# A fused state-space and MLP block on one core: first weights in four pieces, one broadcast held back, the opening of the matmul engine rearranged, and a new hand-written order of all steps

## The chip, the core and the metric

The kernel runs on one core of one Trainium2 chip. The metric is the device time of one execution in microseconds (us), as the median of several runs. One further execution was recorded by the hardware profiler; all durations below come from it.

## What is computed

The input x is one sequence of 2048 rows of 448 numbers in bfloat16. It is normalized once, and the normalized rows go two ways: through a diagonal complex state-space recurrence (a scan over the 2048 rows), and through a second normalization and a two-layer MLP of width 1792. The two are multiplied and added to x.

```python
xn = _layernorm(x, axis=-1)
s = _A_ref(xn, ...)        # Bu = xn @ B_bar.T ; h = Lam_bar*h + Bu ; y = 2*Re(h @ C.T) + xn*Dskip
g = _silu(_B_ref(xn, ...)) # _layernorm(xn), gelu(y @ w1 + b1) @ w2 + b2
return x + s * g
```

## The kernel before, in words

The 2048 rows are cut into eight blocks (x0 to x7) of 256 rows, and a pair of blocks makes a group g = 0 to 3. A partition holds two neighbouring rows of a block (par 0 and 1), so one block is two tiles of 128 rows. The recurrence is run over pairs of rows: 256 steps per group, each step advancing two rows.

Per group the work is this. The statistics of the four tiles are taken on VectorE (lines 357 and 361), turned into two scales and two offsets (`ln_scale`, lines 388 to 412; on GpSimd for groups 1 to 3, as five instructions with a power function, or on VectorE as eleven small ones), and applied (line 421 on VectorE or 422 on ScalarE) to give xn (for the recurrence) and xm (for the MLP). Both are turned by transposing DMAs on SyncE's queue (`xt`, line 435, shown at line 83) into xnT and xn2T. Only block 0 and the MLP side of block 1 are transposed on TensorE instead (lines 379 and 437). Then TensorE makes: `bu` (line 613), the input of the recurrence, in four parts i = 0 to 3; `mm1` (line 683), the first MLP layer, in seven parts j = 0 to 6 of two times 128 hidden units, each followed by a gelu on ScalarE (690); `mm2` (line 714), the second layer, in four tiles, each followed on VectorE and ScalarE by lines 717, 718 and 719; and `ym` (lines 746, 749 and 752), the output of the recurrence, in four tiles, each followed on VectorE by lines 755 and 758 and by the output DMA. The recurrence (`ssm`, lines 627 to 672) is a long VectorE chain between `bu` and `ym`: three wide products and sums, seven scans (638), three wide ones again; the last results h and hh are what `ym` reads. For group 0 `mm1` is done in halves, one block at a time (`mm1_half`, line 699), so that it can begin as soon as block 0 is there.

Before the loops, small parameters are made (`parameters`, mostly on GpSimd), B is scaled and transposed (`lb` line 564/566 and `bt` line 582, giving the tiles BT0 to BT6), C is loaded and transposed (`ldc`, `ct_dma`, giving Cr) and combined into CQ and CZ (`cq`, again lines 564/566), and M0 is made from CQ (`m0`, line 602). The vector b2 and the skip vector (dbc) are broadcast to all partitions by two DMAs that GpSimd issues (lines 336 and 337); dbc is then halved (338).

w1 (448 x 1792) is loaded in two halves of columns, each as a piece of 384 rows and one of 64 rows (`ldw1`); `fcol` picks the 128 columns of one part with a stride of 7, which fits how w2 is loaded, seven rows to a partition and half. Row 64 of the last quarter of w1_sb holds b1.

Nothing is scheduled while the kernel runs. Every step is a `Task` with the names that it reads and writes. `link` derives what must come before what; `emit` writes the steps to the engines' queues in the order of the list `ORDER`, so an engine does its steps strictly in the order of that list, and waits at a step until what it needs is done. `SECOND` lists the steps that may run on either of two engines and take the second one. The numbers `dur` and `prio` in the code are not used by `emit`; they belong to the program that searched the order. The steps are numbered as the code adds them, so a change that adds steps renumbers all later ones.

In the opening, TensorE does 28 dummy products of the identity (line 777), nine tiny ones for the parameters (453 to 457), eight more dummies, the eight transposes of block 0, and then `mm1_half`. SyncE issues, in order: x0 in two pieces, w1 first half in two pieces, b1, x1, w1 second half in two pieces, B in four, w2 in two, x2 and x3 in one, C in three, and then the transposing DMAs.

The rule by which TensorE's steps in the opening are made:

```python
for n, each, rd, pri in ((28, 0.1, [], 2 * PINNED), (8, 0.06, ["ps7"], 2 * PINNED + 1)):
    pe([lambda e: e.matmul(psum[:, 3, 0:128], ident[:, :], ident[:, :], start=True, stop=True) for _ in range(n)],
       ["ident"] + rd, ["ps3"], n * each, pri)
```

Of the kernel before, what the change touches and what calls it, by code (L numbers as in the profile page):

```python
# [8 lines left out]
ALU = mybir.AluOpType  # L9
# [130 lines left out]
def dram_ap(t, offset, ap):  # L140
    return bass.AP(tensor=t.tensor, offset=offset, ap=ap)
# [5 lines left out]
0 11 18 22 12 1 9 10 19 23 14 83 16 20 24 17 2 15 5 21 25 13 27 3 26 7 8 85 6 28 4 86 29 91 40 87 30 92 84 88 93 31 89 41 94 32 43 42 44 90 48 97 95  # L147
45 33 49 47 96 50 34 59 99 108 46 51 100 110 57 109 101 102 98 35 103 52 112 58 111 53 114 113 39 137 104 116 115 105 176 140 136 106 60 117 138 55 61
118 56 139 107 177 54 141 62 120 175 146 63 119 148 67 163 64 122 142 164 65 144 68 121 161 124 69 66 147 123 71 149 126 77 150 125 81 70 152 143 128
78 154 72 74 127 153 130 73 151 129 79 36 162 132 131 303 82 155 134 75 302 76 178 266 80 307 133 305 135 309 165 167 304 145 308 306 168 310 270 179  # L150
267 156 166 171 181 169 157 172 274 180 158 170 37 314 311 315 271 316 159 312 227 160 313 278 268 38 183 272 269 282 228 275 173 273 182 285 229 317
279 318 186 174 283 280 362 230 281 184 392 320 284 231 363 321 188 286 276 364 185 232 287 277 235 319 233 365 236 366 187 234 395 237 322 368 245
367 241 189 191 243 370 369 244 192 193 323 240 371 194 195 372 197 413 324 415 374 419 417 373 196 199 200 325 375 412 416 414 203 380 418 198 420
326 204 201 238 215 239 327 202 246 213 216 205 248 421 422 328 376 424 425 219 430 206 220 255 223 256 431 257 329 214 258 259 207 381 330 224 388
377 382 208 427 383 378 242 428 379 249 247 209 250 426 389 251 252 217 253 390 384 218 254 423 210 260 221 261 222 211 262 225 472 332 212 226 474
263 473 264 385 265 331 386 288 475 333 338 476 336 334 341 478 477 289 335 342 480 479 339 340 344 482 387 337 481 391 345 291 346 343 290 347 348
349 484 350 483 292 429 293 351 393 295 352 485 356 502 357 394 294 490 296 190 358 353 354 355 359 360 297 298 491 492 486 299 361 432 523 522 526
527 525 398 487 529 488 524 528 489 433 530 399 493 494 300 434 396 505 400 397 531 534 535 401 495 536 532 496 540 435 402 541 403 405 503 404 436
497 504 537 301 538 437 406 539 600 408 438 407 441 439 542 442 498 440 533 443 446 543 450 447 449 570 544 451 448 545 571 499 455 456 444 457 453
445 458 572 452 459 460 409 546 467 574 461 573 410 462 463 466 464 454 465 547 468 575 469 576 411 470 548 471 500 552 578 577 551 553 549 579 556  # L160
580 550 561 558 582 581 554 555 559 508 501 583 562 560 564 584 557 509 563 510 506 603 511 566 585 588 512 586 513 587 507 565 515 567 568 592 589
514 569 590 516 517 591 596 593 601 594 602 595 518 597 598 609 519 599 606 520 610 521 604 611 613 605 607 608 612 617 614 621 615 618 616 619 622
620 623 624
""".split()]
SECOND = [int(k) for k in """
138 141 142 143 167 171 173 197 199 217 223 284 311 318 320 393 395 396 421 422 424 425 428 503 505 506 507 532 534 535 538 541 603
# [12 lines left out]
def bass_recurrent_scan__ssm_conv_s5__mixer_channel_mlp__prompt_kernel(  # L179
# [18 lines left out]
    with ExitStack() as es:  # L198
# [63 lines left out]
        def pool(fn, reads=(), writes=(), dur=0.3, prio=0):  # L262
            kb.add("pool", fn, reads, writes, dur=dur, lat=0.15, prio=prio)
# [7 lines left out]
        def pe(fn, reads=(), writes=(), dur=0.2, prio=0):  # L271
            kb.add("pe", fn, reads, writes, dur=dur, lat=0.25, prio=prio)

        with nc.Block():
# [28 lines left out]
            def ld(eng, o, i, writes, nbytes, prio, reads=(), dur=0.45):  # L303
                kb.dma(eng, o, i, reads=reads, writes=writes, prio=prio, nbytes=nbytes, dur=dur)
# [8 lines left out]
            NW1 = 2  # L313

            def ldw1(c, prio):
                w = F // NW1
                ld("sp", w1_sb[:, 0:3, c * w:(c + 1) * w],
                   dram_ap(B_w1, c * w, [[F, 128], [128 * F, 3], [1, w]]), [f"w1_{c}"], 384 * w * 2, prio, dur=0.55)
                ld("sp", w1_sb[0:64, 3, c * w:(c + 1) * w], dram_ap(B_w1, 384 * F + c * w, [[F, 64], [1, w]]),
                   [f"w1r_{c}"], 64 * w * 2, prio)  # L320
# [7 lines left out]
            ldw1(1, S1 + 3)  # L328
# [4 lines left out]
            for q in range(2):  # L333
                ld("sp", w2_sb[:, q * 7:q * 7 + 7, :],
                   dram_ap(B_w2, q * 7 * 128 * D, [[7 * D, 128], [D, 7], [1, D]]), [f"w2_{q}"], 650000, S1 + 6, dur=1.7)
            ld("pool", b2bc[:], dram_ap(B_b2, 0, [[0, 128], [1, D]]), ["b2bc"], 114688, -50, reads=["sgn3"])
            ld("pool", dbc[:], dram_ap(A_Dskip, 0, [[0, 128], [1, D]]), ["dbc"], 114688, -20, reads=["b2bc"])
            pool(lambda e: e.tensor_scalar(dbc[:], dbc[:], 0.5, None, op0=ALU.mult), ["dbc"], ["dbc"], 0.8, -20)
# [10 lines left out]
            def xk(b):  # L349
                return [f"x{b}"] if b else ["x0p0", "x0p1"]  # L350
# [13 lines left out]
            def first_norm():  # L364

                for par in range(2):
# [13 lines left out]
                                                                       ident[:, :]) for d in range(4)], [f"xm0p{par}", "ident"], [f"ps{bank}"], 0.33, 2 * PINNED)  # L380
# [293 lines left out]
            def fcol(fi):  # L674

                q, t = divmod(fi, 7)
                return slice(q * 896 + t, q * 896 + 896, 7)

            def mm1(g, j, prio):
# [6 lines left out]
                w = F // NW1  # L686
                cs = sorted({(2 * j * 128) // w, ((2 * j + 2) * 128 - 1) // w})
# [5 lines left out]
            def mm1_half(j, b, k3, prio):  # L693
# [9 lines left out]
                w = F // NW1  # L703
                ws = sorted({(2 * j * 128) // w, ((2 * j + 2) * 128 - 1) // w})
# [5 lines left out]
            def mm2(g, b, par, prio):  # L710
# [5 lines left out]
                pe(fns, [f"gT{gb}_{fi}_{b}" for fi in range(NF)] + ["w2_0", "w2_1"], [f"ps{bk}"], 2.66, prio)  # L716
# [16 lines left out]
            def ym(g, b, par, prio):  # L733
# [9 lines left out]
                def part(c0, c1):  # L743
# [7 lines left out]
                    else:  # L751
# [6 lines left out]
                    dve(lambda e: e.tensor_tensor(o_sb[:, ob, par * D + c0:par * D + c1], t3[:, fb, c0:c1], res, ALU.add),  # L758
                        [f"t3{fb}_{c0}", f"t3{fb}_256"] + ([f"xr{b}"] if par else xk(2 * g + b)), [f"o{ob}_{par}_{c0}"], 0.1 + (0.28, 0.47)[par] * w / D, prio)
                    if last:  # L760
                        kb.dma("sp", dram_ap(out, off + par * D + c0, [[2 * D, 128], [1, w]]), o_sb[:, ob, par * D + c0:par * D + c1], reads=[f"o{ob}_{par}_{c0}"],
                               writes=[f"out{g}{b}{par}{c0}"], prio=prio, nbytes=256 * w)
# [13 lines left out]
            for n, each, rd, pri in ((28, 0.1, [], 2 * PINNED), (8, 0.06, ["ps7"], 2 * PINNED + 1)):  # L776
                pe([lambda e: e.matmul(psum[:, 3, 0:128], ident[:, :], ident[:, :], start=True, stop=True) for _ in range(n)],
                   ["ident"] + rd, ["ps3"], n * each, pri)
# [85 lines left out]
```

## Time and profile before

| what | value |
|---|---|
| median of 4 runs | 161.85 us (161.48 to 162.73) |
| the profiled execution's own time | 162.0 us |
| its span | 160.2 us |
| TensorE busy (line "PE") | 151.9 us, 95% |
| VectorE busy (DVE) | 132.9 us, 83% |
| ScalarE busy (ACT) | 92.7 us, 58% |
| GpSimd busy (POOL) | 56.6 us, 35% |
| TensorE clock granted | 0.999 |
| read from memory | 6.89 MB |

Times in the views are counted from the start of the span. In the views of an engine a row gives the start, the length, the engine and line, the operation, what it writes and reads, how many instructions were merged, and in brackets how long the engine stood idle just before and what ended that. "SPq" is SyncE issuing a DMA: the length of such a row is the issue, not the transfer. A view of one line or tile also gives the time from issue to landing. Rows overlap a little, because an instruction's start and the end of the one before are recorded in pipelined form. Line 83 and line 84 are the helper lines of all transposing and all other DMAs, so their rows are told apart by the tile. "xn_sb" in a row can be xn or xm, "w_sb" w1 or w2, "tmp" also the output tile.

### The profile page before, as it was taken

Reading aid. Unit: us, or ns where it says so; the run is one execution under the profiler, and the core shown is the slowest. Engines: PE = TensorE matmul, PEld = TensorE weight load, DVE = VectorE, ACT = ScalarE, POOL = GpSimd, SP = SyncE. Lnnn points to the kernel's source line nnn. Section 1 sums busy time; section 2 is a strip of 40 time slices with the busy share of each in tenths; the row PEclk is TensorE's granted clock in tenths of the full one; section 3 lists DMA queues with packets and bytes.
Section 4 is the critical chain, followed back from the end, with each engine's and each line's share of the span. In section 5 each row is a group of like instructions: output and inputs, shape, how many; then the busy total and the mean of one; then the engine's idle time right before and its main releaser. Section 6 shows DMA issues by size and latency. Waiting matters only on the chain.

```text
span 160.2 us, 2700 instructions
## 1 busy us (share of the span) xinstructions
PE 151.9 (95%) x944; PEld 97.8 (61%) x944; DVE 132.9 (83%) x254; ACT 92.7 (58%) x152; POOL 56.6 (35%) x132
## 2 busy tenths in 40 slices
PE   6899999959999999999999999999999999999990
PEld 6789955646666665555565556567677665555560
DVE  5588878469799899699993999997989899896763
ACT  3769897949887894956289211344279678111100
POOL 5568939098200433300012843632046000005230
PEclk9999999999999999999999999999999999999999
DMA  4999999999882006000000811062601000010021
GB/s 99 339 322 383 265 157 202 115 141 178 158 151 76 0 0 131 4 0 0 0 0 16 214 34 29 0 179 58 123 4 57 0 4 0 3 54 0 27 87 59
DMA packets 29926, 14.70 MB, mean 92 GB/s; under 512 B 24597, under 2 KB 29593, under 8 KB 29914
## 3 DMA queue, kind: packets, MB, share of 16 engines
q1 hardware_dynamic: 29810, 14.31, 39.9%
q0 software_dynamic: 96, 0.23, 1.1%
q8 instruction: 7, 0.11, 0.3%
q14 instruction: 5, 0.04, 0.1%
q10 hardware_dynamic: 8, 0.00, 0.0%
HBM read 6.89 MB, written 1.84 MB: 54 GB/s over the span
## 4 chain that ended last, share of the span: by engine, by line
PE 74%; DMA 12%; DVE 4%; SPq 4%; POOL 2%; issue 1%; ACT 0%; DVEq 0%
PE psum L683 23%; PE psum L714 20%; PE psum L613 12%; PE psum L746 12%; DMA x_all<-in_A_x_dram 8%; SPq L84 4%; DMA xn2T<-xn_sb 4%; PE psum L749 4%; PE psum L602 3%; DVE lnst L357 1%; POOL lnw L400 1%; DVE t L755 1%; PE psum L752 1%; DVE xn_sb L421 1%; DVE tmp L758 1%
## 5 line engine op out<-in xcount | busy, mean ns | idle before, releaser
L714 PE MATMUL psum<-w_sb,gT 128*128 128x448 bf16 x224 | 44.5, 352 | 0.0
L683 PE MATMUL psum<-xn2T,w_sb 128*128 128x512 bf16 x168 | 38.1, 380 | 1.8 <-DMA xn2T<-xn_sb 1.8
L714 PEld LDWEIGHTS psum<-w_sb,gT 128*128 128x128 bf16 x224 | 21.8, 98 | 19.4
L683 PEld LDWEIGHTS psum<-xn2T,w_sb 128*128 128x128 bf16 x168 | 21.8, 132 | 15.0 <-DMA xn2T<-xn_sb 2.1
L690 ACT ACTIVATE gT<-psum 128x1024 bf16<-128x1024 f32 x21 | 21.5, 1022 | 11.5 <-PE psum L683 11.4
L613 PE MATMUL psum<-xnT,BT 128*128 128x256 bf16 x196 | 24.0, 273 | 0.0
L613 PEld LDWEIGHTS psum<-xnT,BT 128*128 128x128 bf16 x196 | 19.0, 98 | 5.4 <-ACT u_sb L617 0.5
L718 ACT ACTIVATE th<-o 128x448 f32<-128x448 f32 x16 | 9.1, 573 | 20.6 <-DVE o L717 20.5
L755 DVE TENSOR_TENSOR t<-psum,g_sb 128x448 bf16<-128x448 f32 (+2 forms) x17 | 10.1, 592 | 5.6 <-PE psum L752 3.9
L638 DVE TENSOR_TENSOR_SCAN s_f<-cw,cur,v_sb 128x256 f32<-128x256 f32 x21 | 14.4, 734 | 0.2
L719 DVE SCALAR_TENSOR_TENSOR g_sb<-th,o 128x448 bf16<-128x448 f32 x16 | 10.9, 683 | 4.3 <-ACT th L718 4.3
L699 PE MATMUL psum<-xn2T,w_sb 128*128 128x256 bf16 x112 | 12.8, 273 | 0.9 <-DVE xn2T L381 0.6
L730 POOL TENSOR_TENSOR xr<-xd,g_sb 128x448 f32<-128x448 bf16 x4 | 4.5, 1120 | 24.8 <-DVE g_sb L719 20.9
L699 PEld LDWEIGHTS psum<-xn2T,w_sb 128*128 128x128 bf16 x112 | 12.1, 132 | 1.3 <-DVE xn2T L381 0.8
L421 DVE TENSOR_SCALAR xn_sb<-x_all,lnw 128x448 bf16<-128x448 bf16 x20 | 10.3, 534 | 2.1 <-POOL xd L730 1.4
L746 PE MATMUL psum<-CZ,h_sb 128*128 128x448 bf16 x56 | 11.9, 352 | 0.0
L717 DVE TENSOR_TENSOR o<-psum,b2bc 128x448 f32<-128x448 f32 x16 | 9.9, 618 | 1.7 <-PE psum L714 1.6
L617 ACT ACTIVATE u_sb<-psum 128x512 bf16<-128x512 f32 x12 | 7.1, 592 | 6.8 <-PE psum L613 6.8
L746 PE MATMUL psum<-CQ,h_sb 128*128 128x448 bf16 (+2 forms) x54 | 10.5, 332 | 0.0
L422 ACT ACTIVATE xn_sb<-x_all,lnw 128x448 bf16<-128x448 bf16 x10 | 7.5, 755 | 5.1 <-DVE xn_sb L421 3.7
L357 DVE BATCH_NORM_STATS2 lnst<-x_all 128x6 f32<-128x448 bf16 x14 | 8.2, 611 | 1.9 <-DMA x_all<-in_A_x_dram 1.9
L706 ACT ACTIVATE gT<-psum 128x512 bf16<-128x512 f32 x14 | 8.1, 594 | 2.5 <-PE psum L699 2.4
(154 smaller groups left out, 222.6 us busy)
## 6 DMA issues: line engine op xcount, KB each, us to landing
w_sb<-in_B_w_dram SPq DMA_DIRECT2D x2, 784.0 KB, 9.3
out_dram<-tmp SPq DMA_DIRECT2D x7, 224.0 KB, 1.9
w_sb<-in_B_w_dram SPq DMA_DIRECT2D x2, 672.0 KB, 5.6
x_all<-in_A_x_dram SPq DMA_DIRECT2D x3, 448.0 KB, 3.8
gT<-in_A_C_re_dram SPq DMA_DIRECT2D x1, 392.0 KB, 13.0
Bn<-in_A_B_re_dram SPq DMA_DIRECT2D x1, 336.0 KB, 6.6
Bn<-in_A_B_im_dram SPq DMA_DIRECT2D x1, 336.0 KB, 6.7
gT<-in_A_C_im_dram SPq DMA_DIRECT2D x1, 336.0 KB, 12.9
```

The lines of the kernel that those rows point to most:

```text
L357: dve([lambda e, b=b, par=par, q=q: e.bn_stats(lnst[:, q, :], x_all[:, 2 * g + b, par, :])], [f"x{2 * g + b}"] + (["xmT0p1"] if (g, b) == ...
L421: on = [("dve", lambda e: e.tensor_scalar(dst, src, rs, nb, op0=ALU.mult, op1=ALU.add), 0.4, 0.12), ("act", lambda e: e.activation(dst, sr ...
L613: fns = [lambda e, r=r, m=m, d=d: e.matmul(psum[:, 4, r * NK:(r + 1) * NK], BT[:, m, d, :], xnT[:, gx, d, :], start=(d == 0), stop=(d == 6 ...
L638: dve(lambda e, i=i, ri=ri, init=init: e.tensor_tensor_scan(s_f[:, i, ri, :], col(R2, i).to_broadcast([128, NK]), v_sb[:, i, ri, :], init, ...
L683: fns = [lambda e, k=k, d=d: e.matmul(psum[:, b0 + k, :], w1_sb[:, d, fcol(2 * j + k)], rhs[:, d, :, :], start=(d == 0), stop=(d == 3)) fo ...
L690: act(lambda e: e.activation(gT[:, gb, 2 * j:2 * j + 2, :], psum[:, b0:b0 + 2, :], ACT.Gelu_apprx_tanh), [f"ps{b0}", f"ps{b0 + 1}"] + (WK ...
L699: fns = [lambda e, k=k, d=d: e.matmul(psum[:, banks[k], :].rearrange("p (r c) -> p r c", r=2)[:, :, cs], w1_sb[:, d, fcol(2 * j + k)], rhs ...
L714: fns = [lambda e, fi=fi: e.matmul(psum[:, bk, 0:D], gT[:, gb, fi, q * 128:(q + 1) * 128], w2_sb[:, fi, :], start=(fi == 0), stop=(fi == N ...
L717: dve(lambda e: e.tensor_tensor(o2[:, fb, :], psum[:, bk, 0:D], b2bc[:], ALU.add), [f"ps{bk}", "b2bc"], [f"oo{fb}"], 0.62, prio - 76)
L719: dve(lambda e: e.scalar_tensor_tensor(out=g_sb[:, gs, :], in0=th[:, fb, :], scalar=1.0, in1=o2[:, fb, :], op0=ALU.add, op1=ALU.mult), [f" ...
L746: fns = [lambda e, k=k: e.matmul(psum[:, bk, c0:c1], h_sb[:, hb, k, k0:k0 + 128], cm[:, k, c0:c1], start=(k == 0), stop=False) for k in ra ...
L755: dve(lambda e: e.tensor_tensor(t3[:, fb, c0:c1], psum[:, bk, c0:c1], g_sb[:, gs, c0:c1], ALU.mult), [f"ps{bk}", f"g{gs}"], [f"t3{fb}_{c0} ...
```

## The change

Six things are edited.

1. w1 is loaded in four pieces of 4, 4, 4 and 2 times 128 columns (`CH`), each again as 384 and 64 rows; w2 in four pieces to match. `fcol` takes a stride of 4 (2 in the last). A part of `mm1` now waits for its own piece alone; `mm2` waits for all four of w2.
2. The broadcast of b2 also waits for the last piece of w1 (`w1r_3`).
3. The first four transposes follow the parameter products at once, then come five dummies, the other four transposes, and five more dummies. The eight dummies are gone.
4. Halving dbc may run on ScalarE or VectorE instead of GpSimd (it takes VectorE).
5. At the end, the last tile's second addition may run on GpSimd, and its output DMA is issued by ScalarE; the additions of a tile wait for their own part only, where before the first also waited for the second's product.
6. `ORDER` and `SECOND` are new from end to end.

The code, without the two lists:

```diff
-            NW1 = 2
+            CH = ((0, 4), (4, 4), (8, 4), (12, 2))
+            chunk = [c for c, (_, n) in enumerate(CH) for _ in range(n)]
             def ldw1(c, prio):
-                w = F // NW1
-                ld("sp", w1_sb[:, 0:3, c * w:(c + 1) * w],
...
+                a, w = CH[c][0] * 128, CH[c][1] * 128
+                ld("sp", w1_sb[:, 0:3, a:a + w], dram_ap(B_w1, a, [[F, 128], [128 * F, 3], [1, w]]), [f"w1_{c}"], 384 * w * 2, prio, dur=0.55)
+                ld("sp", w1_sb[0:64, 3, a:a + w], dram_ap(B_w1, 384 * F + a, [[F, 64], [1, w]]), [f"w1r_{c}"], 64 * w * 2, prio)
...
-            ldw1(1, S1 + 3)
+            for c in (1, 2, 3):
+                ldw1(c, S1 + 3)
...
-            for q in range(2):
-                ld("sp", w2_sb[:, q * 7:q * 7 + 7, :],
-                   dram_ap(B_w2, q * 7 * 128 * D, [[7 * D, 128], [D, 7], [1, D]]), [f"w2_{q}"], 650000, S1 + 6, dur=1.7)
-            ld("pool", b2bc[:], dram_ap(B_b2, 0, [[0, 128], [1, D]]), ["b2bc"], 114688, -50, reads=["sgn3"])
+            for c, (a, n) in enumerate(CH):
+                ld("sp", w2_sb[:, a:a + n, :], dram_ap(B_w2, a * 128 * D, [[n * D, 128], [D, n], [1, D]]), [f"w2_{c}"], 98000 * n, S1 + 6, dur=0.5 + 0.1 * n)
+            ld("pool", b2bc[:], dram_ap(B_b2, 0, [[0, 128], [1, D]]), ["b2bc"], 114688, -50, reads=["sgn3", "w1r_3"])
...
-            pool(lambda e: e.tensor_scalar(dbc[:], dbc[:], 0.5, None, op0=ALU.mult), ["dbc"], ["dbc"], 0.8, -20)
+            kb.either(("act", lambda e: e.activation(dbc[:], dbc[:], ACT.Copy, scale=0.5), 0.6, 0.2),
+                      ("dve", lambda e: e.tensor_scalar(dbc[:], dbc[:], 0.5, None, op0=ALU.mult), 0.2, 0.12), ["dbc"], ["dbc"], -20)
...
+                    pe([lambda e: e.matmul(psum[:, 3, 0:128], ident[:, :], ident[:, :], start=True, stop=True) for _ in range(5)],
+                       [f"xm0p{par}", "ident"], ["ps3"], 0.3, 3 * PINNED + 1)
...
-                q, t = divmod(fi, 7)
-                return slice(q * 896 + t, q * 896 + 896, 7)
+                a, n = CH[chunk[fi]]
+                return slice(a * 128 + fi - a, (a + n) * 128, n)
...
-                    dve(lambda e: e.tensor_tensor(o_sb[:, ob, par * D + c0:par * D + c1], t3[:, fb, c0:c1], res, ALU.add),
-                        [f"t3{fb}_{c0}", f"t3{fb}_256"] + ([f"xr{b}"] if par else xk(2 * g + b)), [f"o{ob}_{par}_{c0}"], 0.1 + (0.28, 0.47)[par] * w / D, prio)
+                    add = lambda e: e.tensor_tensor(o_sb[:, ob, par * D + c0:par * D + c1], t3[:, fb, c0:c1], res, ALU.add)
+                    rd = [f"t3{fb}_{c0}", f"t3{fb}_256"] if c0 == 0 and not (last and par) else [f"t3{fb}_{c0}"]
...
+                    if last and par:
+                        kb.either(*on, rd, [f"o{ob}_{par}_{c0}"], prio)
...
-                        kb.dma("sp", dram_ap(out, off + par * D + c0, [[2 * D, 128], [1, w]]), o_sb[:, ob, par * D + c0:par * D + c1], reads=[f"o{ob}_{par}_{c0}"],
+                        kb.dma("act" if c0 else "sp", dram_ap(out, off + par * D + c0, [[2 * D, 128], [1, w]]), o_sb[:, ob, par * D + c0:par * D + c1], reads=[f"o{ob}_{par}_{c0}"],
...
-            for n, each, rd, pri in ((28, 0.1, [], 2 * PINNED), (8, 0.06, ["ps7"], 2 * PINNED + 1)):
+            pe([lambda e: e.matmul(psum[:, 3, 0:128], ident[:, :], ident[:, :], start=True, stop=True) for _ in range(28)],
+               ["ident"], ["ps3"], 2.8, 3 * PINNED)
```

Counted out step by step, the new lists give these queues, as far as the prediction speaks of them. SyncE: x0, w1 piece 0, b1, x1, w1 pieces 1 to 3, B in four, w2 in four, x2 and x3, two of the three pieces of C, then the transposes BT3, the last piece of C, xnT of block 1, BT0, xnT of block 0, xm of block 2, xm of block 3, the four of C, x4 and x5, BT4, BT1, x6 and x7, BT5 and so on. TensorE after the opening: `mm1_half` for block 0 (the transposes of block 1 behind part 5), for block 1, the four `mm2` of group 0, one `bu` of group 0, all seven `mm1` of group 1 in a row, the next `bu` of group 0, three `mm2` of group 1, and then `m0`, `bu`, `mm2` and `mm1` of group 2 by turns up to the first `ym`. GpSimd: the b2 broadcast now stands in front of 20 small parameter steps and the broadcast of dbc directly behind them, where before the scales of group 1 stood in front of it. VectorE: the scales of group 1 (moved from GpSimd), all four xm of group 1, the halving of dbc, and the recurrence of group 0, which now stands behind nearly all of CQ and CZ. At the end TensorE makes the smaller part (columns 256 to 447) of the last tile before the larger.

## Prediction

> **What bounds the kernel now.** I read the page first: the engines' shares, then the slices.
>
> ```profile
> PE 151.9 (95%) x944; PEld 97.8 (61%) x944; DVE 132.9 (83%) x254; ACT 92.7 (58%) x152; POOL 56.6 (35%) x132
> ...
> PE   6899999959999999999999999999999999999990
> ...
> DVE  5588878469799899699993999997989899896763
> ...
> PEclk9999999999999999999999999999999999999999
> DMA  4999999999882006000000811062601000010021
> ```
>
> TensorE is busy from start to end, at full clock, with a dip in the ninth slice; transfers fill the first twelve slices. So the time is TensorE's work plus the places where it does not run, plus what comes after it. TensorE's timeline names the places:
>
> ```profile
> 5.15 1.03 PE L777 MATMUL psum<-ident 128*128 128x128 bf16 x8
> 5.98 0.82 PE L379 MATMUL psum<-ident,xn_sb 128*128 128x128 bf16 x8
> 7.42 2.83 PE L699 MATMUL psum<-xn2T,w_sb 128*128 128x256 bf16 x24 [0.63 <-DVE xn2T L381]
> 10.55 1.93 PE L699 MATMUL psum<-xn2T,w_sb 128*128 128x256 bf16 x16 [0.30 <-DMA w_sb<-in_B_w_dram]
> ...
> 36.22 1.94 PE L683 MATMUL psum<-xn2T,w_sb 128*128 128x512 bf16 x8 [1.78 <-DMA xn2T<-xn_sb]
> ```
>
> Useful work starts at 7.42; then it stops 0.30 us for the second half of w1 and 1.78 us for the transposed xm of group 1; after 38 us the waits list no stop of TensorE over 0.2 us. How that transpose came late is in SyncE's and GpSimd's timelines:
>
> ```profile
> 14.07 7.00 SPq L83 DMA_TRANSPOSE xnT<-xn_sb  x1
> ...
> 28.60 3.40 SPq L83 DMA_TRANSPOSE xn2T<-xn_sb  x2
> 32.05 4.14 SPq L83 DMA_TRANSPOSE BT<-Bn  x2
> ```
> ```profile
> 27.69 0.64 POOL L84 DMA_DIRECT2D dbc<-in_A_Dskip_dram  x1
> ```
>
> The first transpose was stuck 7 us in its issue, until the loads had drained at 21. A transpose otherwise takes 1.3 us of issue and lands after 3.0 to 3.3; the two for xm of group 1, issued just after the dbc broadcast, landed after 6.0 and 6.3. The broadcast itself lands at 32.2.
>
> The end, in VectorE's timeline:
>
> ```profile
> 154.87 0.62 DVE L755 TENSOR_TENSOR t<-psum,g_sb 128x448 bf16<-128x448 f32 x1 [1.10 <-PE psum L749]
> 155.53 0.39 DVE L758 TENSOR_TENSOR tmp<-t,x_all 128x448 bf16<-128x448 bf16 x1
> 155.84 0.42 DVE L755 TENSOR_TENSOR t<-psum,g_sb 128x256 bf16<-128x256 f32 x1
> 156.29 0.42 DVE L758 TENSOR_TENSOR tmp<-t,xr 128x256 bf16<-128x256 bf16 x1
> 156.75 0.36 DVE L755 TENSOR_TENSOR t<-psum,g_sb 128x192 bf16<-128x192 f32 x1
> 157.14 0.36 DVE L758 TENSOR_TENSOR tmp<-t,xr 128x192 bf16<-128x192 bf16 x1
> ```
>
> Six VectorE steps without a pause, then an output DMA.
>
> **The opening.** The parameter products end at 5.15, and the first tile is normed at 4.75 (VectorE: 4.39 plus 0.36). So its transposes run 5.15 to 5.57 (eight took 0.82). Five dummies at 0.104 (eight filled 5.15 to 5.98) reach 6.09, the second four transposes 6.50. Before, transposes ended at 6.80 and the work began at 7.42, so 0.62 later; now 7.12 to 7.15. Gain **0.27**. Dummies behind the last transposes lie in the wait for the copy. Ends: 0 if weights or b1 are then late, 0.5 if the copy of the first tile, now off that path, shortens it more.
>
> **w1 in four pieces.** Six more issues on SyncE (four of w1, two of w2) at about 0.48 us: B moves 1.9 us back, x2 and x3 from 8.27 to about 11.1. Is that paid? Bytes in the order of issue: x0 0.23 MB, piece 0 0.46, x1 0.23, pieces 1 to 3 1.15, B 0.8, w2 1.6, x2 and x3 0.46. The stretches show 0.40 MB moved by 4 us, 1.75 by 8, 3.04 by 12, 4.2 by 15, 5.0 by 17. By 8.4 us 2.6 MB are issued and 1.9 moved; at 11 all 4.5 MB, against 2.7 moved. The queue does not run dry: cost 0. Pieces land 1.0 to 1.4 us behind their bytes (w1's second half: 2.06 MB pass at 8.9, landed 10.3). So piece 1 lands near 8.1 and is needed at 8.9 (two parts of 0.88), piece 2 near 9.7 against 10.7, piece 3 near 10.4 against 12.9. The 0.30 goes: gain **0.30**. Against this stands the Trainium skill, "DMA: Bandwidth & Descriptors", section "Rules for kernel authors": for bandwidth, at least 1 MiB per DMA, and its measured table gives 64 KB a third of the peak. If each of six more DMAs paid the 2.0 us which that page fits as fixed, one behind the other, x2 and x3 would land 12 us later. The rows say otherwise: the stretches of 1 us between 4 and 14 us move 237 to 401 GB/s with pieces of 56 to 784 KB in the queue, because several are in flight. I take 0; bounds -0.3 to +1.0. A weight load with stride 4 in place of 7 I leave at 0: the matmuls go 0.109 us apart at stride 7, as line 613's do at contiguous weights (14 in 1.53).
>
> **b2 held back, and the GpSimd queue.** The wait ends about 10.4. In GpSimd's queue the broadcast stands behind the sine chain and four more steps, which ended near 13.5 in the trace, so nothing waits. Queued behind it are 20 small steps, 0.8 us later for its issue; only CQ and CZ need them, at 37. It is issued near 14 instead of 19.8, and its user (line 717) needs it at 22.7. Cost 0. Behind these, dbc is issued at about 21.6 instead of 27.7.
>
> **Group 1's xm, the big term.** Moved: scales from GpSimd (24.02 to 27.73, 3.7 us) to VectorE (eleven instructions, 8.95 to 10.95, 2.0 us). With x2 and x3 landed by 20 to 20.8, four statistics (2.35) and aggregates end at 23.5, line 717 24.1, scales 26.1, first two xm 26.9, line 717 again, last two xm 28.3. SyncE: drained at 20.5 to 21, then BT3, last piece of C, xnT, BT0, xnT reach 26; xm of block 2 issues at 27, of block 3 at 28.4 to 29.7, lands **31.6**. TensorE: 7.15 plus 12.3 (fourteen halves) plus 0.5 (transposes) is 20.0; four `mm2` at 2.65 reach 30.6; one `bu` 32.2. So undisturbed the stop is 0. But the dbc broadcast now lies upon BT3 and xnT: before, such a collision held SyncE's queue 0.85 plus 1.5 us (issues of 2.12 and 2.80 in place of 1.3). Moved ahead whole, landing is 34.0 and the stop 1.9; yet b2's broadcast before, issued at 19.8, let transposes issued from 21.2 land after 3.5 to 4.0, almost free. Two rows far apart; I take the middle, a stop of **1.0**, gain **0.78**, and keep 0 to 2.5.
>
> **Middle.** Seven `mm1` in a row, then from 33.1: `mm1` 12.1, `bu` 1.53, three `mm2`, `m0` 1.4 and so on put the first `ym` at 80.1. VectorE by then has the recurrence of group 0: from line 717 at 49.4 its 47 steps sum to 27.7 (four times 0.55, eight sums at 0.66, seven scans at 0.70, six wide steps at 0.95, and so on) plus 1.3 waiting: 78.4. Spare 1.7. Vector work rises 2.0 for the scales and 0.3 for its other swaps. I allow **+0.2** for small stops along the new order; ends 0 and 3.3.
>
> **The end.** Order now: product 448, product 192, sum 448, product 256, sum 256; the sum of 192 goes to GpSimd and its DMA to ScalarE's queue. The distances in the trace make 0.66 + 0.39 + 0.35 + 0.45 + 0.42 = 2.27 instead of 2.63; the last DMA is the larger (landing 1.6 for 1.5). GpSimd: 1.03 for 448 columns, so some 0.5 from 155.9, ScalarE's DMA before SyncE's. Gain **0.30**; ends 0.4 and, if GpSimd and VectorE block each other, -0.2.
>
> Sum: -0.27 - 0.30 - 0.78 - 0.30 + 0.20 = -1.45 on the profiled execution's 162.0 (span 160.2 and 1.8 around it). The median is 161.85, 0.15 less: **160.4**.
>
> **Rivals.**
> 1. *Collision in full* (0.19). The stop for xm stays at 2.0 and nothing is won there: 160.4 + 1.0 = 161.4. For it: 6.0 and 6.3 us landings beside dbc; against: b2's mild case. The change then does not do its main thing.
> 2. *VectorE late for group 0's recurrence* (0.25), the slower side. One mechanism: GpSimd does the scales of group 3 between 70 and 74 and the state's carry behind, and wide VectorE steps stretch beside GpSimd: line 667 took 1.79 at 89.3 and 0.95 at 69.8. Six such steps cost 5.0; less the 1.7 spare, TensorE stands 3.3 before the first `ym`: 163.7. With half of them 162.0 to 162.8. It decides once h and hh end after 80.1. For it: VectorE has no pause from 54 on; against: before, GpSimd did its large steps apart and VectorE's sizes held within 5% between 49 and 80. The Trainium skill ("SBUF — State Buffer", section "SBUF: two separate sides") makes the pair of ports an exclusive lock per instruction: the wide step would wait for a whole GpSimd instruction (0.2 to 1.7 here), so few meetings, but long ones.
> 3. *No stop at all* (0.12): 160.4 - 1.2 = 159.2.
>
> The forecast itself has 0.44, with 159.8 to 161.0. Faster by over 0.5% (about what a measurement of this kernel can tell) is under 161.04: 0.44 + 0.12 = 0.56. Rival 1 and a mild third of rival 2 lie within: 0.19 + 0.07 = 0.26. The rest of rival 2, over 162.66, is slower: 0.18. Range 159.2 to 163.0.
>
> **What would show it.** First line-699 product at 7.1, not 7.4; no stop for w1; x2 and x3's landing not after 21; dbc issued at 21 to 22; the wait before the first line-683 product between 0 and 2; no stop before the first line-746 product, near 80; five VectorE steps at the end over 2.3 us. Wrong if x2 and x3 land later than 22 (queue ran dry), if a `bu` waits for BT or xnT, or if h of group 0 ends after TensorE arrives.

## The result, and the profile after

The changed kernel takes 159.87 us (median of 27 runs, 159.44 to 161.55), the kernel before 161.4 us (median of 36 runs beside them, 159.88 to 165.28). The ratio is 0.9928, with a 95% interval of 0.9908 to 0.9948: 0.7% faster, some 1.2 us. The forecast was 160.4. Ratios and intervals, here and below, are of the runs that lie within 1.5% of their kernel's fastest, medians are of all runs, and the profiled executions of two variants (the scales back on GpSimd, and the kernel before with its first transposes ahead) lie above those 1.5%, so that nothing rests on their traces alone.

The profiled executions differ more: 162.0 and 159.9 us, spans 160.2 and 158.1. The one of before lies 0.6 above its median, so of the 2.1 us that the traces explain below, part is that execution's own. Lines from 380 on have moved by one to three.

The page of the changed kernel: busy times, slices of TensorE and of the transfers, and the chain that ended last.

```profile
PE 151.5 (96%) x946; PEld 93.9 (59%) x946; DVE 136.9 (87%) x265; ACT 93.1 (59%) x151; POOL 52.4 (33%) x127
...
PE   6979999999999999999999999999999999999990
...
DMA  4999999889950057000200430204511000010032
...
PE 92%; DMA 3%; SPq 2%; DVE 1%; issue 0%
```

TensorE's busy time hardly moved (151.9 before); the dip in the ninth slice is gone, and one stands in the third. TensorE's timeline names both places:

```profile
5.26 0.44 PE L382 MATMUL psum<-ident 128*128 128x128 bf16 x5
...
6.77 1.91 PE L701 MATMUL psum<-xn2T,w_sb 128*128 128x256 bf16 x16 [0.28 <-issue]
9.56 3.69 PE L701 MATMUL psum<-xn2T,w_sb 128*128 128x256 bf16 x32 [0.88 <-DMA w_sb<-in_B_w_dram]
...
20.68 10.76 PE L715 MATMUL psum<-w_sb,gT 128*128 128x448 bf16 x56
...
32.80 3.40 PE L686 MATMUL psum<-xn2T,w_sb 128*128 128x512 bf16 x15
```

The first product came 0.65 us earlier (6.77 for 7.42). But the second piece of w1 had not landed: the stop for w1 is 0.88 instead of 0.30, and the second layer begins at 20.68, where it began at 20.62. The opening won nothing. The row of line 686 has no bracket: the stop of 1.78 us for group 1's xm is gone.

How much that is can be read from the table by stretch, cut where the second layer begins, where group 1's first layer begins and where the six last VectorE steps begin (columns: length, TensorE's busy time and instructions, granted clock, share of the transfers, GB/s). Before:

```profile
20.62:36.20 15.58, 13.81 (x86) 1.00 1.15 153
36.20:154.87 118.67, 118.61 (x676) 1.00 0.23 52
sum 134.25, PE 132.42; mean PE 66.21
```

After:

```profile
20.68:32.80 12.12, 12.12 (x72) 1.00 1.26 170
32.80:153.07 120.27, 120.20 (x693) 1.00 0.25 54
sum 132.39, PE 132.32; mean PE 66.16
```

The same work, 132.4 and 132.3 us, took 134.25 us before with 1.83 idle, and takes 132.39 now with 0.07 idle. (One `bu` has changed its place across the cut, so only the sums compare.) The long middle is thus TensorE's work and nothing else, in both.

SyncE's timeline of the changed kernel, and GpSimd's with the broadcast of dbc:

```profile
18.89 1.33 SPq L83 DMA_TRANSPOSE BT<-Bn  x1
...
20.91 2.21 SPq L83 DMA_TRANSPOSE xnT<-xn_sb  x1
...
27.01 2.97 SPq L83 DMA_TRANSPOSE xn2T<-xn_sb  x2
```
```profile
21.12 0.61 POOL L84 DMA_DIRECT2D dbc<-in_A_Dskip_dram  x1
```

The two transposes of xm are issued 1.6 and 1.2 us earlier (27.0 and 28.7) and land after 3.7 and 3.3 us instead of 6.0 and 6.3, at 30.7 and 32.0; they are needed at 32.8. Those before them, beside the broadcast, land after 5.1 to 5.9.

The end, all engines but TensorE:

```profile
153.07 0.89 DVE L756 TENSOR_TENSOR t<-psum,g_sb 128x448 bf16<-128x448 f32 x2 [0.69 <-PE psum L750]
...
153.88 0.38 DVE L759 TENSOR_TENSOR tmp<-t,x_all 128x448 bf16<-128x448 bf16 x1
...
154.04 0.62 POOL L759 TENSOR_TENSOR tmp<-t,xr 128x192 bf16<-128x192 bf16 x1 [2.52 <-DVE t L756]
154.34 0.42 DVE L756 TENSOR_TENSOR t<-psum,g_sb 128x256 bf16<-128x256 f32 x1
154.69 0.38 ACTq L84 DMA_DIRECT2D out_dram<-tmp  x1
154.80 0.42 DVE L759 TENSOR_TENSOR tmp<-t,xr 128x256 bf16<-128x256 bf16 x1
```

From the first step to the end of the last is 2.15 us, for 2.63 before; from the first step to the end of the span 5.03 for 5.33.

The account of the two executions: up to the second layer +0.06, idle in the middle -1.76, TensorE's work -0.10, end -0.30; together -2.10, the difference of the spans.

### The profile page after: what moved, and what is told of

Same layout as the page of the kernel before. It is cut to its first block, busy times and chain, and to the rows that moved or that the text cites. A ratio compares the mean times of both kernels' runs of the same rounds, so it can differ in the third digit from the quotient of the medians.

```text
span 158.1 us, 2725 instructions
## 1 busy us (share of the span) xinstructions
PE 151.5 (96%) x946; PEld 93.9 (59%) x946; DVE 136.9 (87%) x265; ACT 93.1 (59%) x151; POOL 52.4 (33%) x127
## 4 chain that ended last, share of the span: by engine, by line
PE 92%; DMA 3%; SPq 2%; DVE 1%; issue 0%
PE psum L715 27%; PE psum L686 23%; PE psum L616 14%; PE psum L747 12%; PE psum L701 7%; PE psum L750 4%; PE psum L605 3%; DMA w_sb<-in_B_w_dram 3%; SPq L84 2%; PE psum L753 1%; PE psum L440 0%; DVE t L756 0%; DVE tmp L759 0%; PE psum L607 0%
## 5 line engine op out<-in xcount | busy, mean ns | idle before, releaser
L715 PE MATMUL psum<-w_sb,gT 128*128 128x448 bf16 x224 | 43.8, 352 | 0.0
L686 PE MATMUL psum<-xn2T,w_sb 128*128 128x512 bf16 x168 | 38.6, 379 | 0.1
L686 PEld LDWEIGHTS psum<-xn2T,w_sb 128*128 128x128 bf16 x168 | 18.5, 112 | 16.0 <-ACT gT L692 1.0
L641 DVE TENSOR_TENSOR_SCAN s_f<-cw,cur,v_sb 128x256 f32<-128x256 f32 x21 | 15.6, 784 | 0.2
L701 PEld LDWEIGHTS psum<-xn2T,w_sb 128*128 128x128 bf16 x112 | 11.8, 112 | 2.0 <-DMA w_sb<-in_B_w_dram 1.1
L731 POOL TENSOR_TENSOR xd<-xn_sb,dbc 128x448 bf16<-128x448 bf16 x4 | 4.7, 1183 | 24.3 <-DVE dbc L339 13.6
L720 DVE SCALAR_TENSOR_TENSOR g_sb<-th,o 128x448 bf16<-128x448 f32 x16 | 10.4, 665 | 0.7 <-ACT th L719 0.6
L731 POOL TENSOR_TENSOR xr<-xd,g_sb 128x448 f32<-128x448 bf16 x5 | 5.5, 1107 | 14.3 <-DVE tmp L759 14.3
L731 POOL TENSOR_TENSOR xr<-x_all,xr 128x448 f32<-128x448 bf16 x6 | 6.9, 1158 | 9.2 <-DVE xr L732 9.1
```

What stands on the lines that cost most here:

```text
L641: dve(lambda e, i=i, ri=ri, init=init: e.tensor_tensor_scan(s_f[:, i, ri, :], col(R2, i).to_broadcast([128, NK]), v_sb[:, i, ri, :], init, ...
L686: fns = [lambda e, k=k, d=d: e.matmul(psum[:, b0 + k, :], w1_sb[:, d, fcol(2 * j + k)], rhs[:, d, :, :], start=(d == 0), stop=(d == 3)) fo ...
L701: fns = [lambda e, k=k, d=d: e.matmul(psum[:, banks[k], :].rearrange("p (r c) -> p r c", r=2)[:, :, cs], w1_sb[:, d, fcol(2 * j + k)], rhs ...
L715: fns = [lambda e, fi=fi: e.matmul(psum[:, bk, 0:D], gT[:, gb, fi, q * 128:(q + 1) * 128], w2_sb[:, fi, :], start=(fi == 0), stop=(fi == N ...
L720: dve(lambda e: e.scalar_tensor_tensor(out=g_sb[:, gs, :], in0=th[:, fb, :], scalar=1.0, in1=o2[:, fb, :], op0=ALU.add, op1=ALU.mult), [f" ...
L731: kb.either(("pool", lambda e, o=o, i0=i0, i1=i1, op=op: e.tensor_tensor(o, i0, i1, op), 1.37, 0.15), ("dve", lambda e, o=o, i0=i0, i1=i1, ...
```

## The experiments

Two theories were at hand for the gain at xm. B: the broadcast of dbc, moved ahead, no longer lies on the transposes of xm. S: the scales of group 1, made by VectorE, bring xm to SyncE's queue earlier. In the kernel before, both stand in one place of the order, since the broadcast was queued behind the scales. Steps are moved by a statement behind the lists; 36 and 37 are the two broadcasts in the kernel before, 42 and 43 in the one after, 317 the scales of group 1 there. Each kernel was profiled in one execution. The kernel before was run again beside each set of variants, so a ratio is against the runs of its own set, whose medians lie between 161.5 and 161.81.

**Before, with both broadcasts early in GpSimd's queue.**

```diff
-""".split()]
+""".split()]; ORDER.remove(36); ORDER.insert(ORDER.index(67) + 1, 36); ORDER.remove(37); ORDER.insert(ORDER.index(80) + 1, 37)
```

> The kernel before, with one thing of the change alone: GpSimd issues the broadcast of b2 near 14 us and that of dbc near 21.5 us, ahead of the scales of group 1; the scales stay on GpSimd. If the stop of 1.78 us before group 1's first MLP product came from the dbc broadcast lying upon the two xm transposes (theory B), these land after 3 to 4 us instead of 6, the stop falls to under 0.3 and the time by 1.0 to 1.8 us. If it came from the scales taking 3.7 us on GpSimd (theory S), the stop stays at 1.5 or more and the time within 0.3 us.

Measured: 160.86 us, ratio 0.9931 (0.9899 to 0.9963). SyncE's timeline of this kernel, then TensorE's:

```profile
28.58 3.72 SPq L83 DMA_TRANSPOSE xn2T<-xn_sb  x2
```
```profile
34.85 1.94 PE L683 MATMUL psum<-xn2T,w_sb 128*128 128x512 bf16 x8
```

The transposes of xm are issued when they were (28.6 and 29.9), land after 5.0 and 4.8 us instead of 6.0 and 6.3, and the product does not wait. (In this execution the opening lost 0.57 more to w1; with the second layer where it was before, some 0.4 of the stop would have stayed.) In this trace the stretch from the second layer to the last steps takes 132.41 us, as in the changed kernel (132.39). So the move of these two steps takes away the stop, in part because the opening was late. The ratio is that of the whole change, but its interval is wide, and the median fell by 0.6 only, where the change's fell by 1.5. Theory B had put the landings at 3 to 4 us; they stayed near 5.

**After, with the broadcast of dbc made to wait for the scales.**

```diff
-        self.link()
+        self.link(); self.tasks[43].deps.add(self.tasks[317])
...
-""".split()]
+""".split()]; ORDER.remove(43); ORDER.insert(ORDER.index(317) + 1, 43)
```

> The changed kernel, with the dbc broadcast made to wait for the scales of group 1, so that it is issued near 26.2 us, just ahead of the two xm transposes at 27.0 and 28.7. Theory B: they land after 5 to 6 us, near 33 and 34.5, and TensorE stops 1.0 to 1.8 us before group 1's first MLP product; the time rises by as much. Theory S: they land by 32.3 and the time stays within 0.3 us.

Measured: 160.95 us, ratio 0.9991 (0.9969 to 1.0013); the gain is lost. GpSimd's timeline and TensorE's:

```profile
26.50 0.61 POOL L84 DMA_DIRECT2D dbc<-in_A_Dskip_dram  x1 [5.37 <-DVE xn_sb L424]
```
```profile
33.98 3.40 PE L686 MATMUL psum<-xn2T,w_sb 128*128 128x512 bf16 x15 [1.22 <-DMA xn2T<-xn_sb]
```

xm is issued as early as in the changed kernel (26.8 and 28.1), but lands after 6.2 and 5.8 us, and the stop is back. With the scales where the change put them and only the broadcast late, the time is 1.1 us above the changed kernel's, close to the stop of 1.22: B holds in both directions.

**After, with the scales back on GpSimd and the broadcast still early.**

```diff
-""".split()]
+""".split()]; ORDER.remove(43); ORDER.insert(ORDER.index(88) + 1, 43); SECOND.remove(317)
```

> The changed kernel, with the scales of group 1 back on GpSimd (five instructions, 3.7 us in the trace before) and the dbc broadcast still ahead of them. Theory S: xm is ready 1.7 us later, its second transpose lands near 33.7 instead of 32.0, and TensorE, which needs it at 32.8, stops about 0.9 us; the time rises by 0.9. Theory B gives the same lateness but no more than that, since no broadcast lies upon it: 0.5 to 1.0. Were the landing also over 4 us after the issue, something else than the broadcast would delay these transposes.

Measured: 160.11 us, ratio 0.9905 (0.9878 to 0.9932), no loss that can be told from the changed kernel's 0.9928. Both theories had expected 0.5 to 1.0 us, so that missed. Its profiled execution, the longest of the 22 runs, had a long stop for w1 (2.12 us) and one of 0.90 for xm, issued at 29.4; it can't show how the stop would be with the usual opening. By the times, the gain doesn't need S; why the late scales cost nothing is not shown.

All traces together: where dbc was issued 0.3 to 1.9 us ahead of the first transpose of xm (three kernels), the two landed after 5.8 to 6.4 us; where it was not (eleven kernels), after 3.2 to 5.0. What spreads the second group is not shown.

**After, w1 in pieces of 6, 2, 4 and 2.** The stop for w1 comes because the second piece is needed after two parts and lands at 9.5; a first piece of six times 128 columns, three parts, takes that need away.

```diff
-            CH = ((0, 4), (4, 4), (8, 4), (12, 2))
+            CH = ((0, 6), (6, 2), (8, 4), (12, 2))
```

> The changed kernel, with the same columns of w1 cut 6, 2, 4, 2 instead of 4, 4, 4, 2. In the changed kernel TensorE stopped 0.88 us for the second piece, which landed at 9.5. Now three parts of the MLP hang on the first piece and the second is not needed before 9.4. If the stop is a question of which bytes have come (theory of the queue), it goes to under 0.2 and the time falls by 0.5 to 0.9. If later stages swallow what the opening wins (xm of group 1 lands at 32.0, needed then at 32.0; w2 at 18.8), the first stage ends earlier and the time stays within 0.3.

Measured: 159.99 us, ratio 0.9889 (0.9843 to 0.9935). The second layer begins at 19.85, 0.83 earlier, without a stop for w1; but xm lands at 32.8 as ever, and TensorE now waits 0.74 for it. Most of what the opening wins is handed to the next wait.

**Before, with the first transposes ahead of the eight dummies.**

```diff
-""".split()]
+""".split()]; ORDER.remove(84); ORDER.insert(ORDER.index(95) + 1, 84)
```

> The kernel before, with the opening of the change alone: the eight transposes of block 0 stand directly behind the parameter products, the eight dummies behind them. The first half of w1 landed at 7.24 us in the trace before. If the change needs its pieces together with its opening (theory P), the first line-699 product moves from 7.4 to 7.2 or 7.3 only, now held by w1 and not by the transposes, the stop for the second half grows from 0.3 to about 0.5, and the time stays within 0.3 us. If the opening alone is worth what it saves (theory O), the time falls by 0.5 or more.

Measured: 161.35 us, ratio 0.9977 (0.9951 to 1.0003). In its profile the first product stands at 7.54, held 0.30 by b1's load and not by w1 as expected, and the stop for xm is 1.65. An earlier opening alone can't be told from no change.

**After, with 36 instead of 28 dummies**, which delays the opening.

```diff
-            pe([lambda e: e.matmul(psum[:, 3, 0:128], ident[:, :], ident[:, :], start=True, stop=True) for _ in range(28)],
+            pe([lambda e: e.matmul(psum[:, 3, 0:128], ident[:, :], ident[:, :], start=True, stop=True) for _ in range(36)],
```

> The changed kernel with 36 instead of 28 dummy products ahead of the parameter products, so that the first product of the first layer comes some 0.4 to 0.9 us later. If the opening's gain is worth nothing because the second piece of w1 lands when it lands (theory here): the stop for w1 shrinks by as much as the opening got later, the second layer still begins near 20.7, and the time stays within 0.3 us of the changed kernel's 159.9. If the opening is worth its own length: 0.4 to 0.9 us slower.

Measured: 160.21 us, ratio 0.9915 (0.9882 to 0.9948). TensorE's timeline:

```profile
7.83 5.40 PE L701 MATMUL psum<-xn2T,w_sb 128*128 128x256 bf16 x48 [0.28 <-issue]
...
20.67 10.76 PE L715 MATMUL psum<-w_sb,gT 128*128 128x448 bf16 x56
```

The first product is 1.06 us later than in the changed kernel, the 48 run through with no stop, and the second layer begins at 20.67 for 20.68. The time when w1's second piece lands sets the rest, and the new opening's 0.65 us are worth nothing here. The same shows in the changed kernel and in three variants with its cut of w1: TensorE went on with the second piece at 8.88 to 9.56, and began the second layer 11.1 to 11.2 us later in each (20.03 to 20.68). The median is 0.34 above the changed kernel's, between the theory's 0.3 and the rival's 0.4 to 0.9; the ratio shows no loss, so here the trace decides and not the times.

**After, with both broadcasts issued by SyncE at 13.1 and 14.8**, ahead of the transposes; then the same with the pieces 6, 2, 4, 2 (edit as above); then that with the last piece of C (step 184), whose rows are 128 bytes, moved ahead of the broadcasts and the transposes as well. The edit of the first:

```diff
-""".split()]
+""".split()]; ORDER.remove(42); ORDER.insert(ORDER.index(183) + 1, 42); ORDER.remove(43); ORDER.insert(ORDER.index(42) + 1, 43)
...
-            ld("pool", b2bc[:], dram_ap(B_b2, 0, [[0, 128], [1, D]]), ["b2bc"], 114688, -50, reads=["sgn3", "w1r_3"])
-            ld("pool", dbc[:], dram_ap(A_Dskip, 0, [[0, 128], [1, D]]), ["dbc"], 114688, -20, reads=["b2bc"])
+            ld("sp", b2bc[:], dram_ap(B_b2, 0, [[0, 128], [1, D]]), ["b2bc"], 114688, -50, reads=["sgn3", "w1r_3"])
+            ld("sp", dbc[:], dram_ap(A_Dskip, 0, [[0, 128], [1, D]]), ["dbc"], 114688, -20)
```

> The changed kernel, with both broadcasts issued by SyncE behind the loads of x and most of C, near 13 us, and none by GpSimd; nothing else moves. If it is the broadcast from GpSimd's queue that makes transposes land late (theory B), all transposes from the second on land after 3.0 to 3.8 us (in the changed kernel BT3, xnT, BT0 and xnT took 5.1 to 5.9). TensorE did not wait for them there, so the time stays within 0.4 us. If transposes still take 5 us or more, their lateness has another cause than the broadcast's queue.

> The one before, with w1 cut 6, 2, 4, 2 as well. With the cut alone TensorE began its second layer at 19.85 instead of 20.68, but then stopped 0.74 us for the transposed xm, which landed after 4.4 to 4.9 us. Theory B: without a broadcast from GpSimd these land after 3.0 to 3.5, near 31.5, the stop falls to under 0.2, and the time is 0.5 to 1.0 us below the changed kernel's. Otherwise it stays where the cut alone had it.

> The changed kernel with both broadcasts issued by SyncE at 13 to 15 us, w1 cut 6, 2, 4, 2, and the last piece of C, which has rows of 128 bytes, issued ahead of the transposing DMAs instead of between the first of them. If it is that piece which holds the transposes between 18 and 24 us: they land after 3.0 to 3.8 us, group 1's xm is there in time (stop under 0.3 instead of 0.85), and the time is 0.3 to 0.8 us below the 159.5 of the same kernel without the move. If the queue of loads as a whole holds them: same landings and same time.

Measured: 159.90 us, ratio 0.9911 (0.9877 to 0.9945); 159.51 us, 0.9877 (0.9829 to 0.9925); 159.62 us, 0.9884 (0.9845 to 0.9923). In the first of these traces the transposes issued at 18.1 and 20.7 us still land after 6.7 and 5.9, the next two after 3.3 and 3.1, and xm after 4.4 and 4.1 (TensorE stops 0.33 for it). For the first two this does not clear the broadcasts: from SyncE's queue they landed after 10.6 and 9.2 us only, at 23.7 and 24.0, so that they were still in flight. It shows that such transposes are late without a broadcast from GpSimd's queue. For xm, issued 3 us after both had landed, a lateness of about 1 us has another cause than a broadcast, against the expectation of theory B. The piece of C is not it either; with it moved ahead, SyncE's timeline reads

```profile
17.66 4.52 SPq L83 DMA_TRANSPOSE BT<-Bn  x1
```

The first transpose simply sits in its issue until 22.2. In the other variants of the changed kernel, too, the first or the second transpose is held in its issue, for 1.7 to 3.5 us where 1.3 is usual, and free between 22 and 25. That the loads as a whole hold the queue is what is left; no run shows it apart. In the last two kernels the second layer begins at 19.47 and 19.56, and the stop for xm is 0.85 in both.

**After, with the last sum of 192 columns on VectorE.**

```diff
-""".split()]
+""".split()]; SECOND.remove(630)
```

> The changed kernel, with the last tile's smaller sum back on VectorE (its DMA still issued by ScalarE). Six VectorE steps stand at the end again: from the first of them to the last 2.5 to 2.65 us instead of 2.15, so the time rises by 0.2 to 0.5 us. If the end is set by the output's landing and not by VectorE, it stays within 0.1 in the trace's distance from the last-but-one tile's product to the end of the span.

Measured: 160.18 us, ratio 0.9937 (0.9910 to 0.9964). The steps at the end take 2.26 us for 2.15 (2.63 before), and to the end of the span it is 5.1 for 5.03. In the traces the helper engine is worth 0.1 us, and the six steps took less than the 2.5 to 2.65 expected; most of the gain at the end is the order, in which two of the three sums no longer follow directly on the product that they need. The median is 0.3 above the changed kernel's, but the intervals overlap, and this 0.1 does not account for it.

**After, without the hold on b2's broadcast; and after, with one dummy instead of five behind each four transposes.**

```diff
-            ld("pool", b2bc[:], dram_ap(B_b2, 0, [[0, 128], [1, D]]), ["b2bc"], 114688, -50, reads=["sgn3", "w1r_3"])
+            ld("pool", b2bc[:], dram_ap(B_b2, 0, [[0, 128], [1, D]]), ["b2bc"], 114688, -50, reads=["sgn3"])
```
```diff
-                    pe([lambda e: e.matmul(psum[:, 3, 0:128], ident[:, :], ident[:, :], start=True, stop=True) for _ in range(5)],
+                    pe([lambda e: e.matmul(psum[:, 3, 0:128], ident[:, :], ident[:, :], start=True, stop=True) for _ in range(1)],
```

> The changed kernel with the broadcast of b2 no longer waiting for the last piece of w1. Theory: in GpSimd's queue it stands behind the sine chain, which ends near 13, later than the last piece of w1 lands; so its issue stays near 13 and the time does not move (within 0.3 us). Rival: the hold keeps the broadcast out of w1's way; then the broadcast is issued before 12, w1's stop grows, and it is 0.3 to 0.8 us slower.

> The changed kernel with one dummy product instead of five behind each four transposes in the opening. If the dummies only fill time in which TensorE would wait for the copies and for w1: the second layer begins as before near 20.7 and the time stays within 0.3 us. If they keep up the pace of the engine: the first products of the first layer run at about twice the distance (0.2 us instead of 0.11) for a while, and the time is 0.3 to 1.5 us longer.

Measured: 159.72 us, ratio 0.9886 (0.9848 to 0.9923), and 159.55 us, ratio 0.9873 (0.9839 to 0.9907). Neither edit of the change gains anything. Without the hold, b2's broadcast is issued at 14.65, in an execution in which the second layer was 0.84 late; with it at 13.13, though the last piece of w1 had landed at 12.0. It stands behind the sine chain and does not wait for w1. With one dummy the first products keep their length (273 ns) and the second layer begins at 20.48.

Four kernels were measured beside the same runs of before: 36 dummies, no hold, one dummy, and the one with the piece of C moved ahead. Their ratios are 0.9873 to 0.9915, and three of the four intervals reach into the changed kernel's own. None of them is clearly better than the changed kernel. The reason shows in the traces, in us:

| kernel | second layer begins | stop for xm | second xm landed | from second layer to the first of the last steps |
|---|---|---|---|---|
| before | 20.62 | 1.78 | 36.2 | 134.25 |
| before, broadcasts early | 21.19 | 0 | 34.7 | 132.41 |
| after | 20.68 | 0 | 32.0 | 132.39 |
| after, dbc late | 20.47 | 1.22 | 33.9 | 133.70 |
| after, 6 2 4 2 | 19.85 | 0.74 | 32.8 | 133.07 |
| after, 36 dummies | 20.67 | 0 | 32.4 | 132.38 |
| SyncE broadcasts, 6 2 4 2 | 19.47 | 0.85 | 32.4 | 133.19 |

The last column is 132.4 plus the stop, within 0.1. And in the changed kernel's variants with an early broadcast the second xm lands at 32.0 to 32.8 whenever the opening ends at 20.7 or before: a better opening alone can't win more than the 0.8 us by which xm comes before its need.

## Why the prediction held, step by step

The sum was -1.45 us; the traces show -2.10, the medians -1.5, the ratio -1.2. The time was met, in part by luck: the opening and w1 (0.57 together) did not come, xm gave 1.0 more than its term, and the 0.20 set aside for the middle was not lost.

- **The opening, 0.27.** The first product was to come at 7.12 and came at 6.77. The mis-sized term is the distance of transposes and dummies, taken as 0.104 us from before's eight; here five dummies fill 0.44 us, that is 0.055 apart, and the transposes are as close. Nothing of it reached the end, since w1 was then late; the prediction had named that as the lower end ("0 if weights or b1 are then late") and did not choose it.
- **w1 in four pieces, 0.30.** This step failed, both in its sign and in its reason. Piece 1 was to land near 8.1; it landed at 9.5, 5.3 us behind its issue, and the stop grew to 0.88. Pieces 2 and 3 came at 11.0 and 12.0 for 9.7 and 10.4. The prediction took the byte rate of before for the new pieces ("the queue does not run dry: cost 0"). The queue did not run dry, and x2 and x3 landed at 20.6 (20.8 before), but between 3 and 7 us it moved 922 KB where before it moved 1139. Two of these four stretches follow; the numbers are the length, the busy time and instructions of TensorE, its weight loads, VectorE, ScalarE and GpSimd, then the granted clock, the share of the transfers and GB/s. Before, after, and with the cut 6, 2, 4, 2:

```profile
4.00:5.00 1.00, 1.00 (x15) 0.77 (x13) 0.72 (x3) 0.74 (x4) 0.00 (x0) 1.00 1.00 382
5.00:6.00 1.00, 0.94 (x13) 0.86 (x11) 0.40 (x1) 0.85 (x7) 0.59 (x3) 1.00 1.12 335
```
```profile
4.00:5.00 1.00, 1.00 (x15) 0.77 (x13) 0.92 (x3) 0.61 (x3) 0.00 (x0) 1.00 0.94 277
5.00:6.00 1.00, 0.89 (x17) 0.70 (x15) 0.65 (x2) 0.91 (x8) 0.59 (x3) 1.00 0.84 163
```
```profile
4.00:5.00 1.00, 0.89 (x12) 0.62 (x10) 0.70 (x3) 0.74 (x4) 0.00 (x0) 1.00 1.07 403
5.00:6.00 1.00, 1.00 (x15) 0.98 (x14) 0.56 (x2) 0.67 (x6) 0.45 (x3) 1.00 0.99 281
```

  The number of DMAs is not the reason. In the same four microseconds the eight traces with the change's cut moved 922 to 1023 KB, the three with the cut 6, 2, 4, 2 moved 1109 to 1147, with as many DMAs, and the three with w1 in two halves 1083 to 1139. What goes with the loss is the first piece: rows of 1024 bytes, where the other cuts have 1536 and 1792. Whether it is the length of the rows or the size of the piece, no run shows apart. The rule that was weighed against the trace there (the Trainium skill, "DMA: Bandwidth & Descriptors", section "Rules for kernel authors") asks for large DMAs; a fixed cost for each further one, 12 us in all, is not what these traces show (the page's fit is of DMAs issued by GpSimd, these are SyncE's).
- **b2 held back, 0.** Right; taking the hold away changed nothing that could be measured.
- **Group 1's xm, 0.78.** Right in its mechanism; the size was the middle of two rows far apart. The measured gain is 1.78, that of the mild row: xm was issued at 27.0, as worked out, and landed at 32.0, not 31.6 or 34.0. The collision was real: the three transposes issued from 20.9 on landed after 5.1 to 5.9 us, and after 3.3 to 3.8 with dbc late. (Not each time: with one dummy and with 6, 2, 4, 2 the last two of them landed after 3.1 to 3.6 beside the same broadcast.) But what it delays there has time to spare. Rival 1 is out. That the gain hangs on where the broadcast stands, and by the times not on the scales, was not foreseen: the prediction treated the two as one step. (The scales on VectorE are ten instructions, not eleven; their 2.0 us are right.)
- **Middle, +0.20.** Nothing was lost: 132.32 us of work in 132.39. Rival 2, VectorE late for the recurrence of group 0, did not come about. VectorE's timeline of the changed kernel has the last step of hh, TensorE's the first product that reads it:

```profile
78.09 0.29 DVE L673 TENSOR_TENSOR h_sb<-pa 128x256 bf16<-128x256 bf16 x1
```
```profile
80.20 1.49 PE L747 MATMUL psum<-CZ,h_sb 128*128 128x448 bf16 x7
```

  It ended at 78.38 (predicted 78.4), the product began at 80.20 (80.1): 1.8 us to spare (1.7). The three wide steps between 72.5 and 76.1 kept their 0.95 us beside GpSimd's small ones, of which three took 0.77 to 0.92 where the shortest take 0.2. VectorE's busy time rose by 4.0 us, not by the 2.3 of the prediction, all of it beside TensorE's work.
- **The end, 0.30.** Measured 0.30 to the end of the span.

So the result is rival 3's stop of zero (159.2, to which the prediction gave a chance of 0.12) plus the 0.57 of the opening and w1 that did not come. What stays open: why the medians differ by 0.6 us less than the two profiled executions, as only one execution of before was profiled and its stop for xm may be larger than usual; what holds the transposes while loads drain; and why late scales cost nothing.

## What to carry to other kernels

A step that is early somewhere is worth only what the next wait leaves of it: find the transfer that is needed next, and the time when it lands, before counting a gain (here 0.65 us won ahead of a piece of w1 that came at 9.5, and then 0.8 ahead of an xm that came at 32.8). A small transfer from another queue, put down just before transposing DMAs that are on the path, can cost more than a microsecond; move it to where the delayed ones have time to spare. And cut the loads by what is needed first, not evenly: here the size of the first piece decided when TensorE could go on, not the number of pieces.

## What the runs showed of the hardware

**TensorE's pace in the first 10 us is not in the row of the granted clock.** That row says 1.00 throughout. But five dummies of 128 columns fill 0.44 us in the changed kernel's profile (219 ns each, 0.055 apart), and in the profile of the kernel without the hold 0.74 (314 ns each, 0.107 apart), where the parameter products had waited:

```profile
5.13 0.22 PE L456 MATMUL psum<-ident,vrows 4*128 4x4 bf16 x3 [0.53 <-DMA vrows<-in_A_Dskip_dram]
...
6.01 0.74 PE L382 MATMUL psum<-ident 128*128 128x128 bf16 x5
...
7.74 6.34 PE L701 MATMUL psum<-xn2T,w_sb 128*128 128x256 bf16 x48
...
21.52 10.76 PE L715 MATMUL psum<-w_sb,gT 128*128 128x448 bf16 x56
```

The 48 products then take 6.34 us instead of 5.40, since the first run slowly. The table by stretch of the same execution (columns as in the result's table) has seven products in the second microsecond and 11 in the third, at a clock of 1.00 by the row:

```profile
8.70:9.70 1.00, 1.00 (x7) 1.00 1.19 252
9.70:10.70 1.00, 1.00 (x11) 1.00 1.13 298
```

The two distances are those that the Trainium skill gives for a cold and a warm array ("TensorE: Matmul & The Clock Gate", section "Wait — 56ns, not 53.3ns?": 106.7 and 55.6 ns at 128 columns). It is the slow pace that set the second layer back by 0.84 us (21.52 for 20.68), not the wait itself: with 36 dummies the 48 products began later still (7.83 for 7.74), ran at full pace, and the second layer began at 20.67. What brought the slow pace is not shown. It stood behind a late load of parameters here and in one other execution (a wait of 0.86 us, second layer at 22.23); but the kernel before with its first transposes ahead ran as slowly between 8 and 10 us (six and seven products in a microsecond) without such a wait. It may be a part of the spread between runs; no run shows how large a part.

**A pair of dependent VectorE steps has a price that an order can hide.** The same six steps of the same sizes took 2.63 us with each sum right behind its product, and 2.26 with another step between two of the three pairs. Each is one execution's record.
